# Query projection in seven products for eight, G products between FFN units, and a planning pass for ScalarE and VectorE in a linear-attention and FFN kernel

## The chip, the cores and the metric

The kernel runs on one core of one Trainium2 chip. Its inputs are in the chip's memory and its output goes back there. The metric is device time in microseconds (us) from one launch to its end; each figure below that is called a time is such a time, and a span is the stretch from the first to the last instruction of one profiled execution.

## The reference: what is computed

One block of 2048 tokens of width 640 in bf16. The input is normalised; a linear attention with 32 heads of width 20 and an FFN of width 1728 both read the normalised input, and their product is added to the input.

```python
phi = lambda t: jnp.where(t > 0, t + 1, jnp.exp(t)) + 1e-6
xn = _layernorm(x, axis=-1)
q, k, v = split_heads(xn @ wqkv)              # 32 heads of 20
pq, pk = phi(q), phi(k)
kv = jnp.einsum("bhsd,bhse->bhde", pk, v)     # per head, 20 x 20
z = jnp.einsum("bhsd->bhd", pk)
num = jnp.einsum("bhqd,bhde->bhqe", pq, kv)
den = jnp.einsum("bhqd,bhd->bhq", pq, z)[..., None] + 1e-6
s = merge_heads(num / den) @ wo
g = silu(jnp.maximum(xn @ w1, 0) @ w2)
out = x + s * g
```

## The kernel before, in words

Tokens are cut into 16 tiles of 128 (t) and 4 chunks of 512 (j); the width 640 is 5 blocks of 128, the FFN width 13 blocks of 128 and one of 64. The values are never projected: since kv is a sum over tokens, the kernel first makes G = xn^T pk (640 x 640), then kv = wv^T G with a mask for the heads, and then W = kv wo, which is called wf. An output tile is then pq (divided by the denominator) times wf, times the gate g, plus x.

*Stages.* (1) Head: load x, mean and variance on VectorE (`bn`, `aggr`), the inverse root on POOL (`aggr`, L475 and L477), normalised tiles xn on VectorE (L497), transposed into xnT by transfers on SP; key tiles 0 to 7 and the FFN blocks 4, 5, 10, 11, 12 of chunk 0. (2) Middle: key tiles 8 to 15 (`K_mm` L556, exp and relu on ScalarE L569, sum on VectorE in `K_fin`), query blocks (`Q_mm` L609: 128 columns of wq by a chunk; exp L617 and relu L622 on ScalarE, sum L630 and L827 on VectorE), FFN blocks (`H_mm` L658) and FFN units. (3) G, kv and wf. (4) The eight pairs of output tiles: the second FFN product with its gate (`U_steps`), the attention product (`O_steps` or, for tiles 0, 1, 14 and 15, `s_tile` and `s_last` at L1529), multiply (L1517), add of x (L1522) and store.

*Seven products for eight.* A 2 x 2 block product needs eight block products, or seven in the scheme of Strassen and Winograd, which takes four sums of the left and four of the right operand ahead of it and combines results in PSUM after it. `h_unit` (L1036 for the matmuls) does this for the FFN: blocks i and i + 6, two chunks, inner dimension 4 of the 5 blocks; the fifth block is added as plain products, so a unit has 18 matmuls of 512 columns for 20. There are four units for chunks 0 and 1 and six for chunks 2 and 3. `seven` (matmuls at L882, copies at L889) does it for G (two pairs of row blocks, the fifth row block by 32 plain matmuls at L1580), for the second FFN product and for the attention product. Steps of a unit are called s1, s5, s6, s2, s7, s3, s4; between them ScalarE copies results from one PSUM bank to another (L1042, L889) and VectorE adds (L827). A unit holds four of the eight PSUM banks. The sums of the left and right operands are made on VectorE by `h_S`, `h_T`, `g_S`, `g_T1` to `g_T4`, `u_S`, `u_T`, `o_S`, `o_T`; they all call `tt`, L827.

*The denominator.* `z_sum` (L756) and `z_col` (L774) make the sums of the keys, `den` (L786) multiplies all queries by them, VectorE scales it (L790) and takes four reciprocals (`den_rec`, L799). `den_store` (L806) writes them spread out to a buffer scr in the chip's memory, four transfers of 640 KB, one for each chunk; `load_recip` (L815) reads them back, and `divide` (L820) multiplies the queries by them. wf is assembled by ten small transfers on SP (L1335) from tiles that ScalarE and VectorE copied out of PSUM (L1325, L1328).

*What sets the order.* All instructions go through `Sched`. `op`, `group` and `dma` put an instruction, or a group of matmuls with one semaphore count at its end, at the end of its engine's queue, and work out from the keys that it reads and writes what it must wait for. Each engine runs its queue in that order. Before the change the order on every engine is the order of the calls, written out by hand: two FFN units take turns on the two halves of PSUM, with query blocks, plain FFN blocks and key tiles as filling between their steps (`fill_`, `misc`, `qfill`); G's units stand after the last FFN unit.

Of the kernel before, what the change touches and what calls it, by code (L numbers as in the profile page):

```python
# [11 lines left out]
class _Res:  # L12
    __slots__ = ("w", "r", "nread")

    def __init__(self):
        self.w = None
        self.r = {}
        self.nread = 0


class Sched:

    def __init__(self, nc, n_dma_sems):
        self.nc = nc
        self.ops = {E: [] for E in ENGS}
        self.count = {E: 0 for E in CENGS}
        self.gseq = 0
        self.seq_at = {E: [] for E in CENGS}
        self.seq_at_dma = []
        self.vc = {E: {} for E in ENGS}  # L30
        self.vc_at = {E: [] for E in CENGS}
        self.vc_at_dma = []
        self.res = {}
        self.ndma = 0
        self.dma_sem_of = []
        self.dsem_count = [0] * n_dma_sems
        self.dsem_last_k = [None] * n_dma_sems
        self.n_dma_sems = n_dma_sems
        self.allow_unread = set()

# [18 lines left out]
    def _require(self, E, agents, waits):  # L59
        need_eng = {}  # L60
        need_dma = []
        for a in agents:
            if self._known(E, a):
                continue
            if a[0] == "D":
                if a not in need_dma:
                    need_dma.append(a)
            else:
                if need_eng.get(a[0], -1) < a[1]:
                    need_eng[a[0]] = a[1]  # L70
        items = [("E", Ep, idx, self.seq_at[Ep][idx]) for Ep, idx in need_eng.items()] + \
                [("D", a[1], None, self.seq_at_dma[a[1]]) for a in need_dma]
        items.sort(key=lambda x: -x[3])
        for kind, a1, a2, _sq in items:
            if kind == "E":
                Ep, idx = a1, a2
                if self._known(E, (Ep, idx)):
                    continue
                waits.append(("E", Ep, idx + 1))
                vc = self.vc[E]  # L80
                vc[Ep] = max(vc.get(Ep, 0), idx + 1)
                self._merge(E, self.vc_at[Ep][idx])
            else:
                k = a1
                if self._known(E, ("D", k)):
                    continue
                si, val = self.dma_sem_of[k]
                waits.append(("D", si, val))
                self.vc[E][("D", k)] = True
                self._merge(E, self.vc_at_dma[k])  # L90

    def _hazards(self, R, W):
        agents = []
        for key in R:
            st = self.res.get(key)
            if st is not None and st.w is not None:
                agents.append(st.w)
        for key in W:
            st = self.res.get(key)
            if st is not None:  # L100
                if st.w is not None:
                    agents.append(st.w)
                agents.extend(st.r.values())
        return agents

    def _update_res(self, agent, R, W):
        Rset = set(R)
        for key in R:
            st = self.res.get(key)
            if st is None:  # L110
                st = self.res[key] = _Res()
            rk = agent if agent[0] == "D" else agent[0]
            st.r[rk] = agent
            st.nread += 1
        for key in W:
            st = self.res.get(key)
            if st is None:
                st = self.res[key] = _Res()
            else:
                assert (st.w is None or st.nread > 0 or key in Rset or key in self.allow_unread  # L120
                        or (agent[0] == "PE" and st.w[0] == "PE")), (
                    "unread overwrite of %r by %r (prev writer %r)" % (key, agent, st.w))
            st.w = agent
            st.r = {}
            st.nread = 0

    def op(self, E, fn, R=(), W=(), extra=()):
        return self.group(E, [fn], R, W, extra)

    def group(self, E, fns, R=(), W=(), extra=()):  # L130
        assert E in CENGS
        waits = []
        agents = self._hazards(R, W) + list(extra)
        self._require(E, agents, waits)
        idx = self.count[E]
        self.count[E] += 1
        self.vc_at[E].append(dict(self.vc[E]))
        self.seq_at[E].append(self.gseq)
        self.gseq += 1
        self.ops[E].append(("op", waits, fns, idx))  # L140
        self._update_res((E, idx), R, W)
        return (E, idx)

    def dma(self, E, fn, sem_idx, R=(), W=(), extra=()):
        waits = []
        agents = self._hazards(R, W) + list(extra)
        prev = self.dsem_last_k[sem_idx]
        if prev is not None:
            agents.append(("D", prev))
# [14 lines left out]
    def wait_all_dma(self, E, sem_idxs):  # L164
        waits = []
        for si in sem_idxs:
            k = self.dsem_last_k[si]
            if k is None:
                continue
# [1527 lines left out]
```

## Time and profile before

| | |
|---|---|
| time, median of 3 runs | 209.08 us (208.42 to 210.09) |
| span of the profiled execution | 207.0 us |
| PE (TensorE matmul) busy | 203.6 us, 98% |
| DVE (VectorE) busy | 169.7 us, 82% |
| ACT (ScalarE) busy | 124.3 us, 60% |
| POOL (GpSimd) busy | 18.0 us, 9% |
| moved by DMA | 24.74 MB |
| query blocks, L609 | 100 matmuls |
| FFN units, L1036 | 180 matmuls |
| seven-product units, L882 | 612 matmuls |

The profiled execution's own time is not given apart from its span; the three times shown are of other executions of the same program. In the profile, PE is TensorE's matmuls, PEld its weight loads (beside the matmuls), DVE VectorE, ACT ScalarE, POOL GpSimd, and SP the engine whose queue issues most transfers. A line number is a line of the kernel. A matmul's entry lasts longer than the distance to the next one, since matmuls overlap; a stretch divided by the matmuls in it gives what one costs. The chain that ended last is followed back from the last instruction; a wait is put down to what released it.

### The profile page before, as it was taken

How to read it: one execution, taken by the hardware profiler on the slowest of the kernel's cores; microseconds unless marked ns; L12 is line 12 of the kernel's file. 1: busy time of each engine (PE TensorE's matmuls, PEld its weight loads, DVE VectorE, ACT ScalarE, POOL GpSimd, SP SyncE). 2: the span in 40 equal slices, each digit the busy share in tenths (PEclk: the TensorE clock that was granted, in tenths of full speed). 3: DMA queues.
4: the chain of work that ended last, by engine and by line, in shares of the span. 5: the costliest groups of instructions: out<-in, count | busy, mean ns of one | idle time of the engine just before them, and what ended most of it. 6: DMA issues, size and time to landing. Idle time of an engine off the chain costs nothing.

```text
span 207.0 us, 3745 instructions
## 1 busy us (share of the span) xinstructions
PE 203.6 (98%) x1400; PEld 126.3 (61%) x1400; DVE 169.7 (82%) x373; ACT 124.3 (60%) x251; POOL 18.0 (9%) x53
## 2 busy tenths in 40 slices
PE   8999999999999999999999999999999999999995
PEld 7755645545555444444456777777777777777773
DVE  4888997988969787686889669898888989897465
ACT  5598869888889987686563435462525354352531
POOL 3174032101330000000000000000000000000001
PEclk9999999999999999999999999999999999999999
DMA  6965999211037000302225999237931011010103
GB/s 194 331 190 117 255 203 275 42 32 29 6 63 198 25 3 0 127 0 57 74 63 114 251 357 384 90 108 234 371 129 63 3 63 46 21 63 0 63 5 127
DMA packets 32999, 24.74 MB, mean 119 GB/s; under 512 B 12757, under 2 KB 32981, under 8 KB 32981
## 3 DMA queue, kind: packets, MB, share of 16 engines
q1 hardware_dynamic: 31749, 23.13, 39.2%
q10 hardware_dynamic: 1232, 1.37, 1.9%
q8 instruction: 11, 0.18, 0.4%
q14 instruction: 7, 0.06, 0.1%
HBM read 15.81 MB, written 5.24 MB: 102 GB/s over the span
## 4 chain that ended last, share of the span: by engine, by line
PE 97%; DMA 1%; DVE 1%; issue 0%
PE psT L882 40%; PE psT L1036 19%; PE psT L556 11%; PE psT L609 11%; PE psT L658 6%; PE psT L1529 3%; PE psT L1580 2%; DMA reg<-in_A_x_dram 1%; PE psT L676 1%; PE psT L1320 1%; PE psT L530 1%; PE psT L1294 1%; PE psT L756 1%; PE psT L786 1%; PE psT L432 0%; DVE stats L469 0%
## 5 line engine op out<-in xcount | busy, mean ns | idle before, releaser
L882 PE MATMUL psT<-reg,regH 128*128 128x320 bf16 (+1 forms) x224 | 34.3, 299 | 0.0
L882 PE MATMUL psT<-reg 128*128 128x320 bf16 (+1 forms) x164 | 27.7, 299 | 0.0
L882 PEld LDWEIGHTS psT<-reg,regH 128*128 128x128 bf16 (+1 forms) x224 | 21.9, 98 | 8.6
L1354 ACT ACTIVATE wv_sb<-psT 128x320 bf16<-128x320 f32 x28 | 11.3, 436 | 25.2 <-PE psT L882 15.4
L609 PE MATMUL psT<-reg 128*128 128x512 bf16 x100 | 24.4, 379 | 0.0
L1036 PE MATMUL psT<-reg 128*128 128x512 bf16 x80 | 23.2, 379 | 0.0
L827 DVE TENSOR_TENSOR psT<-psT,reg 128x320 f32<-128x320 f32 x30 | 14.3, 493 | 9.3 <-PE psT L882 9.2
L889 ACT ACTIVATE psT<-psT 128x320 f32<-128x320 f32 x32 | 13.6, 426 | 11.2 <-PE psT L882 10.7
L882 PEld LDWEIGHTS psT<-reg 128*128 128x128 f16 (+1 forms) x164 | 16.0, 98 | 6.9 <-DVE regH L827 0.2
L889 ACT ACTIVATE reg<-psT 128x320 f32<-128x320 f32 (+1 forms) x24 | 10.4, 435 | 15.6 <-PE psT L882 13.6
L556 PE MATMUL psT<-reg 128*128 128x320 bf16 x120 | 17.9, 299 | 0.0
L1042 ACT ACTIVATE psT<-psT 128x512 f32<-128x512 f32 x20 | 11.9, 595 | 8.2 <-PE psT L1036 8.2
L569 ACT ACTIVATE regE<-psT 128x640 bf16<-128x640 f32 x24 | 15.6, 706 | 1.9 <-PE psT L556 1.2
L609 PEld LDWEIGHTS psT<-reg 128*128 128x128 bf16 x100 | 9.6, 98 | 11.6 <-issue 0.7
L1048 ACT ACTIVATE regH<-psT 128x512 bf16<-128x512 f32 (+1 forms) x24 | 14.5, 604 | 2.1 <-PE psT L1036 1.8
L556 PEld LDWEIGHTS psT<-reg 128*128 128x128 bf16 x120 | 11.5, 98 | 6.5 <-ACT regE L569 0.5
L469 DVE BATCH_NORM_STATS2 stats<-reg 128x6 f32<-128x320 bf16 x32 | 14.1, 475 | 1.3 <-DMA reg<-in_A_x_dram 1.3
L827 DVE TENSOR_TENSOR reg<-reg 128x1024 f16<-128x1024 bf16 (+6 forms) x17 | 13.5, 805 | 1.7 <-DMA reg<-in_B_w_dram 1.2
L882 PE MATMUL psT<-reg,pqT 128*128 128x320 bf16 (+1 forms) x72 | 14.7, 299 | 0.0
L1517 DVE TENSOR_TENSOR reg<-psT,wv_sb 128x640 bf16<-128x640 f32 (+2 forms) x16 | 11.8, 739 | 3.0 <-PE psT L882 1.8
L1036 PEld LDWEIGHTS psT<-reg 128*128 128x128 bf16 x80 | 7.7, 98 | 9.4 <-issue 0.4
L1522 POOL TENSOR_TENSOR reg<-reg 128x224 bf16<-128x224 bf16 x1 | 0.6, 607 | 144.0 <-DVE reg L1517 144.0
(143 smaller groups left out, 369.0 us busy)
## 6 DMA issues: line engine op xcount, KB each, us to landing
reg<-in_B_w_dram SPq DMA_DIRECT2D x12, 320.0 KB, 5.5
scr<-rden SPq DMA_DIRECT2D x4, 640.0 KB, 8.3
reg<-in_A_x_dram SPq DMA_DIRECT2D x4, 640.0 KB, 6.6
out_dram<-reg SPq DMA_DIRECT2D x15, 160.0 KB, 1.9
regE<-scr SPq DMA_DIRECT2D x3, 640.0 KB, 7.5
reg<-in_A_x_dram SPq DMA_DIRECT2D x4, 320.0 KB, 4.4
reg<-in_A_wo_dram SPq DMA_DIRECT2D x6, 160.0 KB, 3.3
reg<-in_A_x_dram SPq DMA_DIRECT2D x5, 160.0 KB, 5.5
```

Source lines behind the costliest of these rows:

```text
L469: sc.op("DVE", lambda eng: eng.bn_stats(stats[:, t, a, :], xv[:, HN * a:HN * (a + 1)]), R=[("xin", xs(t))], W=[("stats", t, a)])
L556: fns.append(lambda eng, a=a, k=k, lhs=lhs: eng.matmul(ps[b + a][:, 0:HN], lhsT=lhs, rhs=wk[:, k, HN * a:HN * (a + 1)], start=(k == 0), st ...
L569: sc.op("ACT", lambda eng: eng.activation(out=o_.rearrange("p (a n) -> p a n", a=2), in_=ps2(b, HN), func=func, scale=scale), R=[("ps", b) ...
L609: sc.group("PE", [(lambda eng, k=k: eng.matmul(ps[b], lhsT=wq[:, k, P * f:P * (f + 1)], rhs=xnT[:, j, k, :], start=(k == 0), stop=(k == C ...
L658: sc.group("PE", [(lambda eng, k=k: eng.matmul(ps[b], lhsT=w1_col(k, P * f, P), rhs=src[:, k, :], start=(k == 0), stop=(k == C - 1))) for ...
L827: sc.op("DVE", lambda eng: eng.tensor_tensor(out=out, in0=in0, in1=in1, op=op), R=R, W=W, extra=extra)
L882: sc.group("PE", [(lambda eng, k=k, lhs=lhs, rhs=rhs: eng.matmul(ps[b][:, 0:HN], lhsT=lhs, rhs=rhs, start=(start and k == 0), stop=(k == n ...
L889: sc.op("ACT", lambda eng: eng.activation(out=dst, in_=ps[b][:, 0:HN], func=ACTF.Copy), R=[("ps", b)], W=[dkey], extra=extra)
L1036: sc.group("PE", [(lambda eng, k=k, lhs=lhs, rhs=rhs: eng.matmul(ps[b], lhsT=lhs, rhs=rhs, start=(start and k == 0), stop=(k == n - 1), sk ...
L1042: sc.op("ACT", lambda eng: eng.activation(out=dst, in_=ps[b], func=ACTF.Copy), R=[("ps", b)], W=[dkey], extra=extra)
L1048: sc.op("ACT", lambda eng: eng.activation(out=dst, in_=ps[b], func=ACTF.Relu), R=[("ps", b)], W=[("hT", j, f)])
L1517: sc.op("DVE", lambda eng: eng.tensor_tensor(out=tmpo[:, os_, lo:hi].rearrange(shp, a=na), in0=src, in1=g_of(t)[0][:, lo:hi].rearrange(shp ...
```

## The change

1. *Query blocks.* A new `q_unit(f, jp)` makes query blocks f and f + 2 of chunks 2jp and 2jp + 1 in seven products. `h_unit` is split into a common `unit` and its own output rules, and `q_unit` uses the same `unit`: four units take the place of 16 of the 20 query blocks. Four sums of wq are made once (`q_S`), in a part of the hidden buffer that is not yet written. The sums of xnT for both halves of the tokens (`h_T`) now have buffers of their own, the second in the buffer of the input tiles.
2. *G.* The two G units stand between FFN units, and the fifth row block of G is in two parts (`c0`, `c1`), one ahead of the last G unit. Some buffers move with it (`gT4`, the sums of G's second pair, the denominator).
3. *Key tiles 8 to 15* are made by halves of 320 columns in one bank each (`K_half`), with their own exp and relu; the filler matmuls of 192 columns (`whole`, L562) are gone.
4. *Order.* TensorE's order after the head is a written list of steps, `PROGRAM`, of which `a` and `b` are FFN units, `p` and `q` query units, `g` G units, `u` and `o` the second FFN product and the attention product. A step takes free PSUM banks as it comes. `Sched` first records everything; `place` then runs through the program with assumed durations (`cost`, `LAT`, `RATE`), works out for each operation how late it may be for TensorE to keep its order, and fixes the order on ScalarE, VectorE and POOL: of the first 60 recorded operations whose inputs are there, the one that can start first, or one that is due earlier. TensorE and SP keep the recorded order, and the head keeps its own on all engines. `emit` then works out the waits.
5. *Loads.* The load of wv is in two parts, wo is loaded after the FFN units (its buffer now holds sums of xnT till then), the last pair of w2 after the last FFN unit, the stores and reloads of the reciprocals behind them on SP, x for the final add behind the last reload. The denominator's product stands later, after the last FFN unit.
6. *Output.* Tile 14's attention product stands after the last FFN product, right ahead of tile 15's.

The core of the diff:

```diff
-    def h_unit(i, jp=1):
+    def unit(jp, blk, wkeys_, ws, skeys, out, out22, tile=None):
...
+    def q_unit(f, jp):
+        o = P * f
+
+        def out(half, j, b):
+            both, sum_ = Q_evac(j, f + 2 * half, b)
+            both()
+            pend.append(sum_)
+
+        def out22(j, b, s5, skey):
+            tt(ps[b], ps[b], s5, ALU.add, [("ps", b), skey], [("ps", b)])
+            out(1, j, b)
...
+    def K_half(t, a):
+        b = take(True)
+        K_mm(t, [b, b], halves=(a, ))
+        for func, slot, key in ((ACTF.Exp, 0, "ek_e"), (ACTF.Relu, 1, "ek_r")):
...
-        if whole:
-            fns.append(lambda eng: eng.matmul(ps[b][:, HN:512], lhsT=one, rhs=wk[:, 0, 0:512 - HN], start=False, stop=True,
-                                              skip_group_check=True))
...
+    LAT = {"PE": 0.2, "ACT": 0.07, "DVE": 0.07, "POOL": 0.07, "SP": 0.0}
+    RATE = 300e3
...
+    if E == "POOL":
+        return 0.25, 0.3
...
+        for o in reversed(recs):
+            run = o.dur + (o.byt / self.RATE if o.byt else 0.0)
+            o.late = min([recs[s].late - run - self.LAT[o.E] for s in o.succ] + [goal.get(o.n, end - run)])
...
+                    can = [(max(free[E], ready[o.n]), o.late, o.n) for o in w[:self.LOOK] if not nleft[o.n]]
+                    if not can:
+                        continue
+                    est, late, n = min(can)
+                    c = recs[n]
+                    for e2, l2, n2 in can:
+                        if l2 < c.late and (e2 <= est or (e2 < est + c.occ and l2 < est + c.occ)):
+                            c, est2 = recs[n2], e2
...
+PROGRAM = """
+H15 H14 H112 rb LN8 H111 T0 Q04 SQ a0.s5 LN12 a0.s1 H110 SH1 Ka8 a0.s6 a0.s2 p1.s1 p1.s5 a0.s7 a0.s3 p1.s2
+a0.s4 Kb8 p1.s6 Kb9 Ka9 p1.s7 p1.s3 a1.s1 Q14 a1.s5 Ka10 T1 a1.s6 a1.s2 p1.s4 Kb10 a1.s7 hh0 Kb12 a1.s3 a1.s4
...
+q0.s4 b2.s5 g0.s6 g0.s2 g0.s7 b2.s1 g0.s3 b2.s6 b2.s2 zc w2a g0.s4 b2.s7 b4.s5 b4.s1 b2.s3 mv6 b2.s4 b4.s6
+b5.s1 b5.s5 w2b b4.s2 b4.s7 b5.s6 b4.s3 b5.s2 b4.s4 c0 hh1 b5.s3 GS1 w2d g1.s1 b5.s7 g1.s5 b5.s4 w2c dn g1.s6
+g1.s2 g1.s7 wo sl wv1 uSa0 g1.s3 do uSb0 g1.s4 wv0 c1 rc1 uT1 dv0 u0.s1 uT3 uT2 kv0 uT4 kv1 u0.s5 W5 u0.s6
+uSa2 W3 W2 u0.s2 W0 u0.s3 W1 u0.s7 u1.s1 uSa1 W4 dv1 oT u1.s5 u1.s6 u1.s2 u0.s4 uSb1 rc2 oS2 u1.s7 uSb2 u1.s3
+u1.s4 rc3 xre st1 u2.s1 oS1 st0 uSa3 u2.s5 o1.s1 u2.s6 dv3 o1.s5 o1.s2 o1.s6 u2.s2 uSb3 o1.s7 o1.s3 dv2 u2.s7
...
+o6.s5 u7.s2 o6.s2 o6.s6 u7.s7 o6.s7 o6.s3 u7.s3 o6.s4 u7.s4 st14
+"""
...
+    def wo_load():
+        for c in range(VC):
+            r0 = VR * c if c < VC - 1 else D - P
+            dma("SP", lambda eng, c=c, r0=r0: eng.dma_start(wo_sb[:, c, :], A_wo[r0:r0 + P, :]),
+                W=[("wo", c)], extra=norms + hz(hTk))
+
+    def den_out():
+        den_store(0)
+        den_store(1)
+        load_recip(0)
+        den_store(2)
+        den_store(3)
```

In the list, `w2c` and `wo` are loads, `dn` the denominator's product with its reciprocals, `do` the function `den_out`, `rc1` to `rc3` the further reloads, `W0` to `W5` the blocks of wf, `dv` the divides, `st1`, `st0` and `st14` output tiles, `xre` the reload of x.

## The prediction, made before the changed kernel was run

> **What bounds the kernel now.** I read the page's busy shares first, then the chain of work that ended last in order of time, then the busy time of each engine by stage, then the DMA queue of SP.
>
> ```profile
> span 207.0 us, 3745 instructions
> ...
> PE 203.6 (98%) x1400; PEld 126.3 (61%) x1400; DVE 169.7 (82%) x373; ACT 124.3 (60%) x251; POOL 18.0 (9%) x53
> ...
> PE 97%; DMA 1%; DVE 1%; issue 0%
> ```
>
> TensorE carries 97% of the chain. A busy PE could still be a stalled one, so I divide the chain's shares by the counts: L1036 (FFN units, 512 columns) has 18.8% of 207.0 us for 180 matmuls, 216 ns each; L882 (320 columns) 40.2% for 612, 136 ns; L609 (query blocks, 512) 10.5% for 100, 217 ns. Each long group costs the same everywhere, so from 4.5 us to 204.5 us TensorE hardly waits: 200 us of matmuls, 4.5 us ahead, 2.5 us behind. What takes no matmul away cannot help by more than those ends.
>
> ```profile
> 34.97 0.08 PE psT L562
> ...
> 200.82 1.36 PE psT L1529 x10
> 202.18 0.95 PE psT L882 x7
> 203.12 1.39 PE psT L1529 x15
> 204.51 0.02 issue
> 204.53 0.38 DVE reg L1517
> 204.92 0.02 issue
> 204.94 0.37 DVE reg L1522
> ```
>
> (Chain: start, length, what.) The end: tile 14's ten matmuls, a last FFN product, tile 15, then one multiply, one add and the store.
>
> ```profile
> 23.60:90.00 66.40, 66.40 (x385) 32.98 (x383) 55.28 (x140) 54.85 (x102) 8.30 (x22) 1.00 0.37 89
> 90.00:117.00 27.00, 27.00 (x189) 14.55 (x188) 23.07 (x37) 15.62 (x30) 0.00 (x0) 1.00 0.33 83
> 117.00:142.00 25.00, 25.00 (x206) 18.35 (x204) 20.11 (x33) 11.61 (x24) 0.00 (x0) 1.00 0.70 231
> 142.00:207.00 65.00, 62.50 (x465) 45.10 (x463) 52.29 (x112) 24.75 (x65) 0.61 (x1) 1.00 0.26 91
> ```
>
> (Stage: length, then busy PE, PEld, DVE, ACT, POOL, clock, DMA share, GB/s.) VectorE and ScalarE are 83% busy in the first stage while TensorE does not wait: there is room, but little. The clock is 1.00 throughout.
>
> ```profile
> SPq L815 <- DMA scr<-rden: 2.8, 1, 2.8
> ...
> DMA to landing us min/median/max: 5.0/7.7/10.4
> ...
> L1335 SPq DMA_DIRECT2D reg<-reg x10: 552/739/991, 132.5 to 139.4; - x10
> ```
>
> (SP's waits; landing of the transfers of scr; the ten copies that assemble wf.) SP stands still until the reciprocals have landed in scr, and each copy of wf holds it 0.74 us.
>
> **The change, part by part.** Times are of the one profiled execution, span 207.0 us; its own total is not given. The median of the three runs is 2.1 us over the span, which I take to stay.
>
> *Matmuls removed.* Sixteen of the 20 query blocks (80 matmuls at L609) become four units of 18 (72): 8 x 0.216 = 1.73 us. The four 192-column fillers at L562 go: 4 x 0.08 = 0.32 us. Every other matmul is kept, only moved. All of it lies on the chain: -2.05 us.
>
> *Work added beside it.* Each query unit adds three ScalarE copies (row L1042, 0.60 us) and two VectorE adds (row L827, 512 from PSUM, 0.70 us), and four sums of wq at 0.42 us are made once: ScalarE +7.2 us, VectorE +7.3 us. Key tiles 8 to 15 are evacuated by halves, 4 x 0.44 for 2 x 0.71 us: ScalarE +2.8 us. These hide beside TensorE if they fit. In the first 66.4 us of the changed part (it starts at 23.6 us) VectorE had 55.3 us; about 7.0 of the 7.3 us and three G sums of 1.48 us come in: 66.7 us. The three G sums and some 2 us of other G operands are not needed until later, so 60 to 62 us are due, 93% of the stretch. With 83% the wait was nil; at over 100% it would be a microsecond or more.
>
> *The pass.* It fixes each engine's order by times that it assumes. It assumes 0.3 us for a POOL operation; rows L475 and L477 show 0.28 and 0.62 us. So a normalisation may be placed about 0.3 us before its input is there, and what stands behind it on VectorE (the adds that free PSUM) waits too. Eight tiles are open to this: at most 2.4 us of VectorE idle (the row of before shows 1.6 us in four waits). For both effects on TensorE the bounds are 0 (all absorbed) and 3 us; I take 0.4, near the row of before, which cost nothing.
>
> *The loads moved.* TensorE's order is written out in the program, so I added its matmuls up at 136 and 216 ns. The last w2 pair is issued after the last FFN unit, 117.1 us, and needed at 125.6; wo is queued behind it, needed at 128.9; the first part of wv waits for the same unit and is needed at 126.5. Landing was 5.5 (7.7 at most) for w2, 3.3 for wo, 9.0 for all 800 KB of wv, of which this part is 320. All have 8.5 us or more: nothing, and up to 1 us if that cover is gone.
>
> *The reciprocals and SP's queue.* The denominator product moves from 97.4 to 98.5 us to end at 118.0 us, while the first output tile stays at about 142 (141.9 by the sums). Behind it: 0.2 to reach VectorE, 0.69 (L790), 3.5 for four reciprocals (L799): 122.4 us. Then SP has, in this order: stores 0 and 1, reload 0 (waits for store 0), stores 2 and 3, reload 1 (waits for store 1), the ten copies of wf. Store 0 landed 5.6 us after issue before (109.8 to 115.4); so reload 0 at 128.0, issued in 1.6 us, two stores in 1.4, reload 1 in 0.4: 131.4. Ten copies at 0.74: 138.8; the last lands 2.2 later, oT needs 0.49 and the tile about 0.1 more: 141.6, against 141.9. One reciprocal set back by another VectorE operation of 0.7 us uses that up. By the largest row (10.4 for 5.6) it is 4.8 us more. Bounds 0 and 4.5 us; I take 0.5, since the first store is the one whose row applies. The divide, late next, has more room: reload 0 lands 7.4 after 128.0, divide 1.64: 137. Behind reload 3, which waits for divide 1 (reload 1 at 131.4 + 7.4, divide 1.64: 140.5), SP issues the loads of xre; the first lands 6.6 later, about 148, and the adds that read it stand on VectorE. Three buffers hold products until the fourth output tile at 152.8: nothing, up to 2 us if an add stands too early.
>
> *The end.* Tile 14 now stands right ahead of tile 15. Its multiply (0.82) and add (0.48) no longer fall under the 0.95 us FFN product: multiply 14 ends 0.4 us before the last matmul, two multiplies of tile 15 (0.3 each) follow, then add 14, the last multiply (0.38) and add (0.37): the last add ends about 1.3 us after TensorE, where it was 0.8. +0.5 us; bounds 0 (add 14 goes last and its store lands under the other) and 0.9.
>
> *Sum.* -2.05 + 0.4 + 0.5 + 0.5 = -0.65 us: span 206.35, time 208.4 us.
>
> **The rivals.**
>
> *SP's queue holds the first output tile (slower than before).* It decides as soon as reload 1 is issued after about 131.7 us; each later microsecond costs one. For it: the 5.0/7.7/10.4 row, and the 2.8 us for which SP stood before. Against it: the reloads' issue took 0.37 us at the median of three, where I count 1.6. With a store of 8.5 to 10.4 us it costs 2.9 to 4.8 in place of 0.5: 210.8 to 212.7 us.
>
> *VectorE becomes the bound of the first stage.* At 62 us due and the idle of before (11.1 of 66.4 us) cut only by half, 67.6 us are needed for 66.4; with the POOL waits up to 70. It costs 1.2 to 4 in place of 0.4: 209.2 to 212.0 us. Against it: the pass may take any ready operation out of 60, and query sums can be put off.
>
> *Nothing waits.* The hand-made order shows that these engines can be kept behind TensorE; then -2.05 us, 207.0 us. Since 200 us of matmuls less 2.05 are left whatever the order, much less is not possible.
>
> *The clock falls after a long wait.* The opening fillers (L432) loaded weights for 32 matmuls of 128 columns in 3.34 us, 104 ns each; five transposes of the same width later took 0.28 us, 56 ns each: TensorE is at half rate after idling. If the first output tile waits nearly 5 us, a stretch like that one returns and adds 1.7 us: 212.7 + 1.7 = 214.4. [...]
>
> That the change does not do what it says can be left out: the four query units stand in the written program with all their steps.
>
> **How the numbers follow.** Forecast case (small waits, 207.4 to 209.4) 0.58; nothing waits 0.07; VectorE 0.14; SP's queue 0.18; queue and clock 0.03. A measurement here tells about 1% from no change, 207.0 to 211.2 us. Faster needs less than the matmuls allow, so it takes most of the "nothing waits" case and luck: 0.05. Slower: two thirds of the queue's case, the clock, and half of VectorE's: 0.22. The rest, 0.73, is within 1%. The range runs from 206.8 to 212.0 us and leaves out some 0.03 below and 0.09 above; the forecast case alone spans 207.4 to 209.4.
>
> **What would show it.** Right: 1388 matmuls (8 and 4 fewer), chain shares that still give 216 and 136 ns, VectorE over 90% busy in the first 66 us after 23.6, a gap of half a microsecond or none just ahead of the first output tile, and an end some 3 us behind the last matmul. Wrong: TensorE groups with idle ahead of them that name VectorE in the first stage, a copy of wf as the releaser of a gap of over 2 us, a clock under 1.00, or a w2 or wv load as a releaser at 125 us.

## The result, and the profile after

The changed kernel takes 221.68 us (median of four runs, 219.29 to 222.82) where the kernel before takes 208.91: 1.058 times as long, with an interval of 1.051 to 1.065 (a ratio is worked out from the executions, not from the two medians). An execution that fell in a slower state of the chip (here the one of 222.82) is left out of the ratios, and out of the two medians further down that are said to be of three. The forecast was 208.4, within 206.8 to 212.0. The profiled execution has a span of 220.4 us, 13.4 more than before.

The page of the changed kernel:

```profile
span 220.4 us, 3735 instructions
...
PE 206.0 (93%) x1376; PEld 125.1 (57%) x1388; DVE 170.6 (77%) x385; ACT 131.4 (60%) x279; POOL 17.9 (8%) x53
...
PE   8899972999999999999999999959999999999994
...
PEclk9999997699999999999999999997999999999999
...
PE 59%; DMA 15%; DVE 12%; ACT 6%; issue 3%; POOL 2%; SPq 1%; DVEq 0%
```

There are 12 matmuls fewer, as announced (1388 weight loads; some matmul records are missing). But TensorE has fallen from 97% of the chain to 59%, and DMA has risen from 1% to 15%. The slices (5.5 us each) show two holes, in the slices from 33 and from 143 us, and the clock goes down with each. TensorE's waits (line, releaser: us in total, times, longest) and four stretches (length, then busy PE, PEld, DVE, ACT, POOL, clock, DMA share, GB/s):

```profile
PE psT L690 <- DMA reg<-reg: 4.8, 1, 4.8
PE psT L997 <- DVE reg L941: 2.3, 1, 2.3
PE psT L690 <- DMA reg<-in_A_wqkv_dram: 0.9, 1, 0.9
```

```profile
23.60:35.00 11.40, 8.07 (x40) 3.44 (x39) 10.29 (x27) 7.09 (x13) 2.96 (x10) 1.00 1.12 269
35.00:45.00 10.00, 7.76 (x26) 3.37 (x28) 4.22 (x12) 4.38 (x9) 1.82 (x4) 0.66 0.29 47
45.00:90.00 45.00, 44.64 (x246) 22.29 (x249) 39.58 (x98) 40.50 (x90) 3.42 (x8) 1.00 0.12 24
...
142.00:155.00 13.00, 10.73 (x67) 6.98 (x66) 9.16 (x18) 4.19 (x10) 0.00 (x0) 0.87 0.86 260
```

From 45 to 90 us, where most steps of the query units stand, TensorE is 99% busy: the stage that the forecast worried about is not where the time went. A clock of 0.66 over 10 us is 6.8 us at half rate (it reads 0.50 from 35.4 to 42.3 us), of which TensorE worked some 5: 2.5 us lost behind the 4.8 of the wait. A clock of 0.87 over 13 us is 3.4 us at half rate (0.50 from 148.1 to 151.5): 1.7 lost behind the 2.3.

*The first hole.* The chain of the changed kernel (start, length, what):

```profile
26.47 2.71 DMA reg<-reg
...
30.52 6.62 DMA reg<-reg
...
37.19 1.51 PE psT L690 x5
38.70 4.20 PE psT L1170 x11
```

Two transposing transfers (reg<-reg). The one at 26.47 landed in 2.7 us; the one at 30.52 is tile 8's, took 6.6, and key tile 8 (`Ka8`, L690) waits for it. What SP issued ahead of it, in the changed kernel and then in the kernel before:

```profile
23.75 4.00 SPq L679 DMA_TRANSPOSE reg<-reg  x3
27.79 1.60 SPq L513 DMA_DIRECT2D reg<-in_A_x_dram  x3
29.44 1.04 SPq L518 DMA_DIRECT2D reg<-in_B_w_dram  x2
30.52 4.71 SPq L679 DMA_TRANSPOSE reg<-reg  x2
```

```profile
27.48 0.58 SPq L374 DMA_DIRECT2D reg<-in_A_x_dram  x1
28.10 1.21 SPq L546 DMA_TRANSPOSE reg<-reg  x1
29.36 1.11 SPq L374 DMA_DIRECT2D reg<-in_A_x_dram  x2
30.51 1.04 SPq L379 DMA_DIRECT2D reg<-in_B_w_dram  x2
```

Before, tile 8's transposition (28.10) went ahead of the last input tiles and two parts of w1. In the change it is recorded with `LN8`, behind them: 2.4 us later in the queue, and behind 1.3 MB more (four transfers of 320 KB). Its input was there in time; VectorE's normalisation of tile 8 in the changed kernel:

```profile
27.63 0.45 DVE L630 TENSOR_SCALAR reg<-reg,mv,rsy 128x640 bf16<-128x640 bf16 x1
```

*The second hole.* The chain again, 100 us later:

```profile
132.95 5.01 DMA scr<-rden
...
137.98 6.73 DMA reg<-scr
...
144.72 1.56 DVE pqT L934 x2
146.28 0.73 DVE reg L1589
147.02 0.54 DVE reg L941
...
147.61 6.62 PE psT L997 x35
```

Store 0, reload 0, divide 0, a block of wf, then one operand sum (L941, `uSa1`), and only then u1.s5, the second step of the second FFN product. The waiting step does not use the divided queries at all. By the code, `uSa1` writes into the buffer that reload 0 filled, so it must wait until divide 0 has read that.

*The end.* In the changed kernel VectorE has two adds (L1778, the first of them tile 14's) and a multiply left to do after TensorE (L1785, tiles 14 and 15):

```profile
214.22 2.89 PE L1785 MATMUL psT<-reg,pqT 128*128 128x320 bf16 x25
...
217.10 0.83 DVE L1778 TENSOR_TENSOR reg<-reg 128x640 bf16<-128x640 bf16 x1
217.86 0.36 DVE L1773 TENSOR_TENSOR reg<-psT,wv_sb 128x208 bf16<-128x208 f32 x1
218.26 0.38 DVE L1778 TENSOR_TENSOR reg<-reg 128x416 bf16<-128x416 bf16 x1
```

From the last matmul (its entry ends at 217.1) to the end of the span it is 3.3 us, where it was 2.5. The add of tile 14 takes 0.83 us here; the adds of the same size just ahead of it (at 213.5 and 214.7) take 0.48 and 0.49.

### The profile page after: what moved, and what is told of

It is laid out like the page before. It is cut to its first block, busy times and chain, and to the rows that moved or that the text cites. A ratio compares the mean times of both kernels' runs of the same rounds, so it can differ in the third digit from the quotient of the medians.

```text
span 220.4 us, 3735 instructions
## 1 busy us (share of the span) xinstructions
PE 206.0 (93%) x1376; PEld 125.1 (57%) x1388; DVE 170.6 (77%) x385; ACT 131.4 (60%) x279; POOL 17.9 (8%) x53
## 4 chain that ended last, share of the span: by engine, by line
PE 59%; DMA 15%; DVE 12%; ACT 6%; issue 3%; POOL 2%; SPq 1%; DVEq 0%
PE psT L997 26%; PE psT L1170 23%; PE psT L690 4%; DMA reg<-reg 4%; DMA reg<-in_A_x_dram 3%; DMA reg<-scr 3%; DMA reg<-in_A_wqkv_dram 3%; DMA scr<-rden 2%; DVE pqT L934 2%; DVE stats L611 2%; DVE reg L941 1%; PE psT L741 1%; POOL rsy L619 1%; ACT regE L1446 1%; PE psT L793 1%
## 5 line engine op out<-in xcount | busy, mean ns | idle before, releaser
L1170 PE MATMUL psT<-reg 128*128 128x512 bf16 (+1 forms) x139 | 38.6, 388 | 0.4
L997 PE MATMUL psT<-reg,regH 128*128 128x320 bf16 (+1 forms) x224 | 35.3, 301 | 0.6 <-DVE reg L1773 0.4
L997 PE MATMUL psT<-reg 128*128 128x320 bf16 (+1 forms) x172 | 29.1, 303 | 2.3 <-DVE reg L941 2.3
L997 PEld LDWEIGHTS psT<-reg,regH 128*128 128x128 bf16 (+1 forms) x224 | 22.0, 99 | 9.9 <-DVE reg L1773 0.8
L1004 ACT ACTIVATE psT<-psT 128x320 f32<-128x320 f32 x32 | 13.4, 425 | 17.8 <-PE psT L997 15.2
L1170 PEld LDWEIGHTS psT<-reg 128*128 128x128 bf16 (+1 forms) x144 | 14.2, 100 | 17.1 <-issue 1.4
L690 PE MATMUL psT<-reg 128*128 128x320 bf16 x120 | 19.3, 306 | 4.8 <-DMA reg<-reg 4.8
L941 DVE TENSOR_TENSOR psT<-psT,reg 128x320 f32<-128x320 f32 (+1 forms) x33 | 16.6, 512 | 9.1 <-PE psT L997 7.7
L997 PEld LDWEIGHTS psT<-reg 128*128 128x128 f16 (+1 forms) x172 | 16.8, 98 | 10.5 <-DVE reg L941 2.6
L1004 ACT ACTIVATE reg<-psT 128x320 f32<-128x320 f32 (+1 forms) x24 | 10.6, 443 | 18.8 <-PE psT L997 14.7
L690 PEld LDWEIGHTS psT<-reg 128*128 128x128 bf16 x120 | 11.5, 99 | 12.5 <-DMA reg<-reg 5.3
L941 DVE TENSOR_TENSOR reg<-reg 128x1024 f16<-128x1024 bf16 (+6 forms) x24 | 17.1, 722 | 1.9 <-PE psT L1460 1.3
L1177 ACT ACTIVATE psT<-psT 128x512 f32<-128x512 f32 x28 | 17.1, 621 | 1.4 <-PE psT L1170 1.4
L941 DVE TENSOR_TENSOR psT<-psT,wv_sb 128x512 f32<-128x512 f32 x15 | 10.4, 695 | 9.6 <-PE psT L1170 9.5
L1446 ACT ACTIVATE regE<-psT 128x320 bf16<-128x320 f32 x32 | 12.3, 461 | 6.5 <-PE psT L690 6.5
L997 PE MATMUL psT<-reg,pqT 128*128 128x320 bf16 (+1 forms) x72 | 14.3, 299 | 0.0
L1778 POOL TENSOR_TENSOR reg<-reg 128x224 bf16<-128x224 bf16 x1 | 0.6, 606 | 163.4 <-DVE reg L1773 163.4
L1773 DVE TENSOR_TENSOR reg<-psT,wv_sb 128x640 bf16<-128x640 f32 (+2 forms) x16 | 11.6, 735 | 2.4 <-PE psT L997 1.7
L752 ACT ACTIVATE regE<-psT 128x512 bf16<-128x512 f32 x20 | 11.9, 631 | 2.2 <-PE psT L741 1.2
```

The lines of the kernel that those rows point to most:

```text
L690: fns.append(lambda eng, a=a, k=k, lhs=lhs: eng.matmul(ps[bk[a]][:, 0:HN], lhsT=lhs, rhs=wk[:, k, HN * a:HN * (a + 1)], start=(k == 0), st ...
L752: exps.append(sc.op("ACT", lambda eng: eng.activation(out=e_, in_=ps[b], func=ACTF.Exp), R=[("ps", b)], W=[("er_e", es)]))
L941: sc.op("DVE", lambda eng: eng.tensor_tensor(out=out, in0=in0, in1=in1, op=op), R=R, W=W, extra=extra)
L997: sc.group("PE", [(lambda eng, k=k, lhs=lhs, rhs=rhs: eng.matmul(ps[b][:, 0:HN], lhsT=lhs, rhs=rhs, start=(start and k == 0), stop=(k == n ...
L1004: sc.op("ACT", lambda eng: eng.activation(out=dst, in_=ps[b][:, 0:HN], func=ACTF.Copy), R=[("ps", b)], W=[dkey], extra=extra)
L1170: sc.group("PE", [(lambda eng, k=k, lhs=lhs, rhs=rhs: eng.matmul(ps[b][:, 0:nn], lhsT=lhs if tile is None else rhs, rhs=rhs if tile is Non ...
```

## The experiments

Each was timed beside the kernel before, which took 208.4 to 209.2 us; all ratios are to it. A run's time is the median of four executions, or of three where that is said.

### 1. Tile 8's transposition ahead of the loads

```diff
-    x_load(12, 2)
+    LN_norm(8), x_load(12, 2)
...
-        "LN8": lambda: run([(N, 8), (S, 9), (N, 9), (S, 10), (N, 10), (S, 11), (N, 11)]),
+        "LN8": lambda: run([(S, 9), (N, 9), (S, 10), (N, 10), (S, 11), (N, 11)]),
```

> Only SP's order differs from the changed kernel: the transposition of token tile 8 is issued ahead of the loads of x tiles 12 to 15 and two parts of w1, as in the kernel before. Theory 'queue': the 4.8 us for which TensorE waited at 32 us and the half clock behind it (about 2.5 us) go, 221.7 - 7.3 = 214.4 us. Rival 'full engines': VectorE and ScalarE (10.0 and 9.6 of 10 us busy from 55 to 65) cannot follow an earlier TensorE, the wait comes back by 70 us, and at most 3 us are won: 218.7 us or more.

Measured: 214.72 us, ratio 1.031 (1.024 to 1.038). One transposition moved in one queue gives back 7.0 us, about the 4.8 of the wait and the 2.5 of the half clock; the rival ("full engines") falls. Tile 8's transposition is issued at 27.7 and lands 3.6 us later. The second hole is as it was: TensorE's longest wait, and the clock down for 3.4 us behind it.

```profile
PE psT L997 <- DVE reg L941: 2.9, 1, 2.9
```

### 2. The pass told what the transfers really take

The pass assumes about 2 us and the bytes at 300 GB/s for a transfer. Here a store to scr is given a least time of 5.5 us (stores 0 and 1) or 8.0, and a reload 7.0; alone, and together with experiment 1. The order changes on VectorE.

```diff
-                    c.end = line[0] + 0.4
+                    c.end = max(line[0] + 0.4, est + c.floor)
...
-            run = o.dur + (o.byt / self.RATE if o.byt else 0.0)
+            run = max(o.dur + (o.byt / self.RATE if o.byt else 0.0), o.floor)
```

> Only VectorE's order differs: the planning pass is told that a store to scr takes 5.5 or 8.0 us and a reload 7.0 us, as the traces show, so it places the divide later. Theory 'fixed order': VectorE no longer stands 2.7 us in front of the divide with the sums for TensorE behind it, and the wait of 2.3 us at 145 us and the half clock behind it (1.7 us) go: 221.7 - 4.0 = 217.7 us. Rival 'next in line': the first output tile waits for the divide or for wf anyway, and little is won: 220.5 us or more.

> Both edits. If the two waits are apart and nothing else takes their place: 221.7 - 7.3 - 4.0 = 210.4 us. Rival 'full engines': 215 us or more.

Measured: 222.68 us alone, 1.063 (1.056 to 1.070), and 216.85 with the transposition moved, 1.038 (1.035 to 1.041): no gain, rather 1 to 2 us lost, which the intervals do not clearly separate from nothing. u1.s5 still waits 3.0 us. VectorE with the transposition moved:

```profile
138.24 0.82 DVE L1589 CAST reg<-psT 120x640 bf16<-120x640 f32 x1 [0.27 <-PE psT L1584]
138.98 1.55 DVE L934 TENSOR_TENSOR pqT<-pqT,reg 128x1536 bf16<-128x1536 bf16 x2
```

Reload 0 goes out at 130.8 and lands 7.1 us later, at 137.9; the pass has now put both of VectorE's copies of wf (L1589) ahead of divide 0, which therefore starts at 139.0. So VectorE's order has about 1 us of this wait. The other 2 us are the buffer of reload 0: TensorE was at u1.s5 at 138.2, and divide 0 (1.56) with one sum of `uSa1` (0.6) behind a landing at 137.9 ends at 140.1 in any order. The theory that VectorE's fixed order holds `uSa1` falls for that part.

### 3. The denominator earlier

`dn` put ahead of the last step of unit b4, in three forms. First with all four stores right behind it, reload 0 behind the last w2 pair (all these runs include experiment 1):

```diff
-b5.s1 b5.s5 w2b b4.s2 b4.s7 b5.s6 b4.s3 b5.s2 b4.s4 c0 hh1 b5.s3 GS1 w2d g1.s1 b5.s7 g1.s5 b5.s4 w2c dn g1.s6
-g1.s2 g1.s7 wo sl wv1 uSa0 g1.s3 do uSb0 ...
+b5.s1 b5.s5 w2b b4.s2 b4.s7 b5.s6 b4.s3 b5.s2 dn do b4.s4 c0 hh1 b5.s3 GS1 w2d g1.s1 b5.s7 g1.s5 b5.s4 w2c rc0 g1.s6
+g1.s2 g1.s7 wo sl wv1 uSa0 g1.s3 uSb0 ...
```

> Tile 8's transposition ahead of the loads, and the denominator's product with its four reciprocals and stores put ahead of the last step of FFN unit b4, reload 0 behind the last w2 pair. If the wait of 2.9 us ahead of u1.s5 and the half clock behind it come from the chain denominator, store, reload, divide (theory 'chain'), both go: 214.7 - 2.9 - 1.7 = about 210.1 us, clock 1.00. If VectorE or the next load in line (wf's copies, xre, the first output tile) takes their place (rival 'next in line'), a wait of 2 us or more stands within some 15 us of the old one and the time is 213 us or more.

Measured: 222.50 us, 1.065 (1.057 to 1.072), 8 us worse than experiment 1. The wait ahead of u1.s5 is gone; another is there. TensorE's longest wait in this run, and SP's queue:

```profile
PE psT L997 <- DMA reg<-in_B_w_dram: 9.2, 1, 9.2
```

```profile
118.29 5.82 SPq L920 DMA_DIRECT2D scr<-rden  x4
124.16 2.16 SPq L1069 DMA_DIRECT2D reg<-in_B_w_dram  x1
126.36 4.25 SPq L1074 DMA_DIRECT2D reg<-in_B_w_dram  x2
130.66 2.20 SPq L1069 DMA_DIRECT2D reg<-in_B_w_dram  x2
```

SP stood for the reciprocals until 118.3 and then issued 2.6 MB of stores; the last w2 parts (L1074, then L1069), at 115.9 and 119.8 in experiment 1, went out 10 to 11 us later, and the first FFN product waited for them. The rival was right.

Then only store 0 early, and behind the last w2 pair; and then all stores behind wo, so that only the product and the reciprocals are earlier:

```diff
+...b5.s2 dn b4.s4 ... b5.s4 w2c ds0 g1.s6 ... wo sl wv1 uSa0 do g1.s3
```

```diff
+...b5.s2 dn b4.s4 ... b5.s4 w2c g1.s6 ... wo sl wv1 uSa0 do g1.s3
```

> Tile 8's transposition ahead of the loads, the denominator's product ahead of the last step of unit b4 (reciprocals done at about 118), but of the stores only store 0 early, and behind the last w2 pair on SP: issued at about 120.7 us where it was 126.0; it lands at about 126, reload 0 about 133 where it was 138.4. If the wait ahead of u1.s5 hangs on this chain alone (theory), it and its half clock go: 214.7 - 2.9 - 1.7 = about 210.1 us. If any byte ahead of the first FFN product's loads costs as much as it saves (rival: the transfers are the bound here), TensorE waits 2 us or more for a w2 load at about 126, or for the denominators again, and the time is 213 us or more.

> As the run before it (store 0 behind the last w2 pair), but all four stores behind wo, as in the changed kernel: only the denominator's product and the reciprocals are earlier. Store 0 at about 123.6 us where it was 126.0, so reload 0 lands some 2.4 us earlier, and of the wait of 2.9 us some 0.5 is left: theory 210.5 to 212.5 us (the half clock goes unless the last half microsecond brings it). Rival (reciprocals not the start of the chain): the wait stays at 2 to 3 us, 214 to 215 us.

Measured: 215.55 us, 1.028 (1.022 to 1.034), and 214.51, 1.027 (1.022 to 1.031). TensorE's waits in the first and in the second (L997 is u1.s5; L1784 and L1785 are the first output tile):

```profile
PE psT L1784 <- DVE reg L941: 3.0, 1, 3.0
```

```profile
PE psT L1785 <- DVE reg L941: 1.6, 1, 1.6
PE psT L997 <- DVE reg L941: 1.5, 1, 1.5
```

Whole, or in halves: about 3 us of waiting stay, at u1.s5 (2.9 in experiment 1), at the first output tile (3.0), or at both. In the first run reload 0 goes out at 128.8 and u1.s5 does not wait, but store 1 then goes out at 129.2, reload 1 at 136.7, divide 1 follows at 145.4, and the sums for the first output tile stand behind it on VectorE; the clock is down for 3.4 us behind that wait.

### 4. A quarter of the denominators' bytes

This changes the last run of experiment 3 (214.51 us). Each store writes 160 rows for 640 and each reload reads one block of five, which the divide uses for all five; the order is the same on every engine, and the result is not the reference's.

```diff
-        src = rden[H * i:H * (i + 1), :].unsqueeze(1).to_broadcast([H, DH, 512])
+        src = rden[H * i:H * i + 8, :].unsqueeze(1).to_broadcast([8, DH, 512])
...
-        dma("SP", lambda eng: eng.dma_start(Rr[r], scr[:, schunk(i)].rearrange("(m p) s -> p m s", p=P)),
+        dma("SP", lambda eng: eng.dma_start(Rr[r][:, 0:1, :], scr[0:P, schunk(i)].rearrange("(m p) s -> p m s", p=P)),
```

> As the run with the denominator's product early and the stores behind wo (214.5 us), with the same order on every engine, but a quarter of each store and a fifth of each reload of the denominators is moved (160 rows for 640, one block of five), and the divide uses that one block for all five: the output is not the reference's. Theory (the bytes of the denominators in the stretch from 120 to 155 us hold what is left): the two waits of 1.6 and 1.5 us go, 211.0 to 211.9 us. If the dependency costs by its steps and not by its bytes (rival), one of the waits stays at over 1 us: 213 or more.

Measured: 215.18 us, 1.031 (1.027 to 1.035). The theory falls: the denominators' own bytes are not what is left. VectorE of this run (divide 0, then the operands for the first output tile, which wait for a copy of wf):

```profile
136.04 1.56 DVE L934 TENSOR_TENSOR pqT<-pqT,reg 128x1536 bf16<-128x1536 bf16 x2 [0.36 <-DMA reg<-scr]
...
147.70 0.89 DVE L941 TENSOR_TENSOR reg<-reg 128x640 f16<-128x640 bf16 x2 [1.76 <-DMA reg<-reg]
```

Divide 0 starts 1.1 us earlier than with all bytes (137.2), and u1.s5's wait of 1.5 goes (0.5 is left at the step behind it), but the first output tile waits 1.8. Store 0, at a quarter of its size, was still 5.8 us from issue (125.5) to the issue of reload 0 (131.4): 1.6 MB of w2 and wo had been issued in the 4 us ahead of it. Whether these hold it was not tried.

### 5. The copies of wf ahead of reload 1; all blocks of wf on ScalarE

Both change the last run of experiment 3 too.

```diff
-... wv0 c1 rc1 uT1 ... W4 dv1 oT u1.s5
+... wv0 c1 uT1 ... W4 oT rc1 dv1 u1.s5
```

```diff
-        if c in (1, 4):
+        if c in ():
             sc.op("DVE", lambda eng: eng.tensor_copy(dst, ps2(b, HN)[0:n]), R=[("ps", b), ("ps", b + 1)],
```

> As the run with the denominator's product early and the stores behind wo (214.5 us), with reload 1 and divide 1 behind the ten copies of wf instead of ahead of them. Theory (the 1.6 us ahead of the first output tile are SP's order: the copies stand behind reload 1, which waits for store 1): the copies start at about 135.5 and not 137.6, the wait of 1.6 us goes, and 212.9 us is left. Rival (two blocks of wf wait on VectorE behind divide 0, so the copies cannot end earlier, or divide 1 now holds the next tiles): one wait of over 1 us between 139 and 160 stays beside the first, 214 us or more.

> As the run with the denominator's product early and the stores behind wo (214.5 us), with all six blocks of wf copied out of PSUM by ScalarE instead of four by ScalarE and two by VectorE. Theory (the first output tile waits because two blocks of wf stand on VectorE behind divide 0): the last copy of wf is issued some 2 us earlier, the wait of 1.6 us goes, and u1.s5, which stood behind one of those blocks on VectorE, waits 0.7 us less: 212.2 to 212.9. Rival (the copies are late because SP stands behind reload 1): the wait ahead of the first output tile stays at over 1 us, 213.5 or more.

Measured: 216.65 us, 1.040 (1.037 to 1.042), and 214.28 (median of three), 1.031 (1.023 to 1.039). Neither helps. TensorE's waits in the first, and in the second with tile 14 moved (experiment 6; in the profile without that the clock was down for 6.8 us):

```profile
PE psT L997 <- DVE reg L941: 1.8, 1, 1.8
PE psT L997 <- DVE reg L1773: 1.3, 1, 1.3
...
PE psT L1785 <- DVE reg L941: 0.7, 1, 0.7
```

```profile
PE psT L997 <- DVE reg L941: 3.0, 1, 3.0
...
PE psT L1785 <- DVE reg L941: 0.7, 1, 0.7
```

With the copies first, the first output tile waits 0.7 for 1.6, but what stands behind the copies on SP comes later (the loads of x for the adds at 152.2 and not 147.8), and a wait of 1.3 us follows behind a multiply (L1773); the copies begin at 134.3 but still end at 145.5. So neither SP's order nor VectorE's blocks of wf hold the stretch by themselves. What the runs of experiments 4 and 5 share with their base is store 0 at 125 us and divide 0 at 136 to 139.

### 6. Tile 14 ahead of the last step of u7, as before

Tried on five kernels: experiment 2 with the transposition moved, the first form of experiment 3, experiment 4 and both of experiment 5.

```diff
-... o6.s7 o6.s3 u7.s3 o6.s4 u7.s4 st14
+... o6.s7 o6.s3 u7.s3 o6.s4 st14 u7.s4
```

> Both edits, and tile 14 ahead of the last FFN product again, as in the kernel before. Theory: the end behind TensorE's last matmul falls from 3.4 us to the 2.5 us of before, 0.9 us under the run with both edits: 209.5 us. Rival: the end is set by the store's landing and differs by less than 0.3 us.

> As the run with the denominator moved (about 210.1 us), with tile 14's attention product ahead of the last step of FFN unit u7, as in the kernel before. If tile 14's multiply and add then lie under the last product (theory), the stretch behind the last matmul falls from about 3.4 to 2.6 us and the time by 0.5 to 0.9: 209.4. If the waits just ahead absorb it (rival), it is within 0.3 us of that run.

> As the run with a quarter of the denominators' bytes (about 211.4 us; output not the reference's for the same reason), with tile 14's attention product ahead of the last step of unit u7. Theory: the stretch behind the last matmul falls by 0.5 to 0.9 us and the time with it, to 210.7. Rival: the time is the same within 0.3 us.

> As the run with the copies first (212.9 us), with tile 14's attention product ahead of the last step of unit u7. Theory: the stretch behind the last matmul falls from 3.3 to 2.5 us, 212.1. Rival: the time is the same within 0.3 us.

> As the run with all blocks of wf by ScalarE (212.5 us), with tile 14's attention product ahead of the last step of unit u7. Theory: the stretch behind the last matmul falls from 3.3 to 2.5 us, 211.7. Rival: the time is the same within 0.3 us.

Measured: 216.89 us (1.037, 1.032 to 1.041), 221.99 (1.063, 1.059 to 1.068), 213.48 (1.025, 1.022 to 1.028), 215.31 (1.033, 1.029 to 1.038) and 213.84 (1.025, 1.019 to 1.031). Against the same kernel without it: 0.0, -0.5, -1.7, -1.3 and -0.4 us, -0.8 in the mean. In the profiles of the third pair the stretch behind the last matmul is 2.5 us for 3.2, so 0.7 is tile 14's; single pairs lie up to 1 us off that either way, and what made the rest was not traced. The last, at 213.84, is the best version that computes the reference: it is still 2.5% slower than the kernel before.

### 7. Plain query blocks again; no pass

The 16 query blocks as plain products, at the steps s2, s7, s3 and s4 of the units that they replace: on the first form of experiment 3, on its last form, and on experiment 4. And on that first form the pass with a view of one operation.

```diff
-a0.s4 Kb8 p1.s6 Kb9 Ka9 p1.s7 p1.s3 a1.s1 Q14 a1.s5 Ka10 T1 a1.s6 a1.s2 p1.s4 Kb10 ...
+a0.s4 Kb8 Kb9 Ka9 Q03 Q11 a1.s1 Q14 a1.s5 Ka10 T1 a1.s6 a1.s2 Q13 Kb10 ...
```

```diff
-    LOOK = 60
+    LOOK = 1
```

> As the run with the denominator moved (about 210.1 us), but the 16 query blocks are plain products again, 80 matmuls for 72, without the sums of wq, the copies and the adds of the four units. If TensorE is the bound and the eight matmuls count (theory), it is 8 x 0.216 = 1.7 us slower than that run, about 211.8. If the units' work on ScalarE and VectorE in the first stage costs as much as the matmuls save (rival), it is equal or faster: 210.1 or less, with shorter waits on ScalarE or VectorE between 24 and 90 us.

> As the run with the denominator's product early and the stores behind wo (214.5 us), but the 16 query blocks are plain products again: 80 matmuls for 72, no sums of wq, no copies and adds of the units. Theory (TensorE is the bound in the first stage, so the matmuls count): 8 x 0.216 = 1.7 us slower, 216.2. Rival (the run that was 8 us slower without the units showed a real cost of plain blocks, their two exps and relus standing in bursts): 3 us or more slower, 217.5 or more, with waits for ScalarE or VectorE between 30 and 90 us. Third: not slower, 214.5 or less.

> As the run with a quarter of the denominators' bytes (about 211.4 us; output not the reference's for the same reason), with the 16 query blocks as plain products again. With nothing waiting at the denominators, theory: 1.7 us slower than that run, 213.1. Rival: 3 us or more slower. Third: not slower.

> As the run with the denominator moved (about 210.1 us), but ScalarE, VectorE and POOL run in the recorded order behind the head: the planning pass looks at one operation and not at 60. If the pass is needed for this program (theory), TensorE waits for VectorE or ScalarE at many places, 5 to 20 us more: 215 to 230. If the recorded order is good enough by itself (rival), within 2 us of that run: 208 to 212.

Measured, plain blocks: 230.77 us (1.103, 1.094 to 1.112), 221.27 (median of three; 1.067, 1.061 to 1.074) and 219.04 (1.053, 1.049 to 1.057), so 8.3, 6.8 and 3.9 us slower than with the units. By their count the matmuls are 1.7 of that; the wait lists show new waits beside it. The largest of the third run is not at the query blocks but 40 us behind them, at kv (L1558), whose last part of wv ScalarE issued at 129.3 us and not at 121.8, where the whole run stands some 3 us later:

```profile
129.31 0.39 ACTq L518 DMA_DIRECT2D wv_sb<-in_A_wqkv_dram  x1
```

```profile
135.73 1.59 PE L1558 MATMUL psT<-reg,wv_sb 128*128 128x120 bf16 x30 [2.14 <-issue]
```

The reason is again a buffer. ScalarE copies a result of the last G unit (L1004) to one of the places that take turns, in this run and then in experiment 4:

```profile
124.21 0.44 ACT L1004 ACTIVATE wv_sb<-psT 128x320 f32<-128x320 f32 x1 [0.51 <-PE psT L997]
```

```profile
120.86 0.44 ACT L1004 ACTIVATE reg<-psT 128x320 f32<-128x320 f32 x1 [0.51 <-PE psT L997]
```

With the four units gone, the turn falls on the place in wv's buffer; VectorE has read it at 129.3, and then the load goes out. The second run has the same (a wait of 3.3 us at kv). So these 2.1 and 3.3 us are not the price of plain blocks; that price by itself stays open, and nothing contradicts 1.7 us. Without the pass: 278.01 us (1.330, 1.322 to 1.339), beyond the 230 that was expected. This written order needs it.

## Why the prediction was wrong

From the forecast's span without its additions, 204.95 us, to the 220.4 of the profile:

| step | forecast | measured |
|---|---|---|
| matmuls | -2.05 | 12 fewer; not isolated |
| first stage | +0.4 | 0.3 in waits for ScalarE; 1.2 for it and VectorE in experiment 1 |
| loads moved | 0 | +7.0 (experiment 1), the transposition behind them |
| denominators | +0.5 | +4.0: wait 2.3, half clock 1.7 |
| end | +0.5 | +0.8 |

204.95 + 7.0 + 4.0 + 0.8 = 216.75; of the other 3.65 us, the wait list names 2.7 (0.9 for a load in the head, which is 0 to 0.8 in the profiles of the experiments, 0.5 ahead of the first query block, and five smaller ones); 0.95 is not traced.

*"The loads moved: nothing."* This step failed, and it is the larger half. It followed the loads that the description of the change names (w2, wo, wv) to the places where each is needed. It did not list what SP issues in the first 35 us, in the old and the new order. There one line of the diff puts a transposition, needed at 32.4 us, 4.3 after its input was ready, behind 1.3 MB of loads; with these sent after it, in experiment 1, TensorE waits for none of them. The pass could not repair that, since SP keeps the recorded order; and the forecast had no rival with SP in the first stage.

*"The divide, late next, has more room."* This failed too. The chain's own durations were close: in experiment 1 the reciprocals took 3.4 (forecast 3.5), store 0 took 5.0 (5.6), reload 0 took 7.4 (7.4); it all ran some 3 us later, mostly because the product ended at 120.9 and not 118.0. But the deadline was taken from the reader of the divided queries, the first output tile at 141.9. The first to need divide 0 is the writer of its buffer, `uSa1`, and through it u1.s5, which TensorE had reached at 138.4 in experiment 1. A buffer reused is a deadline; it was not looked up. The forecast's own figures show the miss: 49 matmuls of 136 ns lie between u1.s5 and the first output tile, so TensorE is there at about 135.2 by its sums, where divide 0 ends at 137 and a block of wf (0.7) and a sum (0.6) follow it: an estimated wait of 3 us, which experiment 1 has at 2.9.

*SP's queue and the first output tile.* The rival was sound as a mechanism: a wait on u1.s5, some 8 us ahead of the first output tile (experiment 1), hides it. It comes out where that wait is taken away: 3.0 us in the second run of experiment 3, the low end of the 2.9 to 4.8 that it was priced at. Its sum was too short. From the issue of reload 0 to the end of the ten copies of wf the forecast had 10.8 us (128.0 to 138.8); it took 15.0 in experiment 1 (131.0 to 146.0) and in the last run of experiment 3 (131.4 to 146.4), since SP spent 2.6 and 3.5 us on the two stores where 1.4 were counted, 2.3 and 2.1 on reload 1 for 0.4, and 9.3 and 8.8 on the copies for 7.4; what it waited for in each is not worked out here. The first output tile before and in experiment 1:

```profile
142.38 1.52 PE L1529 MATMUL psT<-reg,pqT 128*128 128x320 bf16 x10
```

```profile
149.50 1.52 PE L1785 MATMUL psT<-reg,pqT 128*128 128x320 bf16 x10
```

It starts at 148.0 to 149.5 in the profiles of experiment 1, the second and last runs of experiment 3, experiment 4 and the first run of experiment 5, wherever the waits ahead of it stand.

*First stage and VectorE.* Right in kind. In the last run of experiment 3, VectorE is busy 59.9 of the 66.4 us from 23.6 on (90%; the forecast had 60 to 62 due), and TensorE waits there for VectorE and ScalarE in pieces of 0.5 us and less. (ScalarE's 2.8 us for the halves of the key tiles is 2.7 by the rows given; no term of the sum hangs on it.)

*The end.* Right in kind, short in size: 0.8 for 0.5, near the upper bound. The order was the one forecast; tile 14's add took 0.83 us where 0.48 was counted.

*The clock.* The condition was wrong. A wait of "nearly 5 us" was thought to be needed; it fell behind one of 2.3 us. That length was the author's guess and not shown by the trace of before: TensorE's longest wait there is 0.8 us, and its granted clock reads 1.00 from the start, also where the opening's matmuls took 104 ns for 56. The price of 1.7 us for one such stretch was right.

*The chances.* Slower had 0.22, all from waits in two named places. The changed kernel moved nearly every transfer of SP, and only some were followed; that should have weighed as a case of its own.

What stays open: after experiment 1 some 6 us are left over the kernel before. They lie ahead of the first output tile, which starts some 6 to 7 us later than before; from it to the end of the span experiment 1 takes 63.5 us and the kernel before 64.7. About 3 of them are waits that follow from the denominators' late start (store 0 at 109.8 us before, at 118 to 126 in experiments 1, 3, 4 and 5); they change place and hardly size, since a step let go earlier meets the next wait on the same chain of stores, reloads and copies. By the code, a still earlier product is held by its buffers, in which the changed kernel keeps operand sums for FFN units, and the stores then meet the w2 loads on SP; a version with other buffers was not tried. Nor does any run take back the halves of the key tiles or G's new place, so what these cost or save alone is open.

## What to carry to other kernels

When a change rewrites an order, list each queue's issues before and after, side by side, for every stage, and not only for the transfers that the change speaks of: the 7 us sat in four lines of SP's queue. For each transfer that becomes later, ask who reads the data, and also who next writes the buffer that they lie in. When repairs move a wait of the same size from place to place, look for the common start of their chains, here one product that now stands some 22 us later.

## What the runs showed of the hardware

*The clock halved behind a wait of 2.3 us.* It was down for 3.4 us behind a wait of 2.3 us in the changed kernel and one of 2.9 in experiment 1, for 6.8 behind 4.8. In the changed kernel it reads 0.50 there, and the matmuls of 320 columns followed at 267 ns and not at 136 (seven from 149.0 us on). Behind a wait of 3.0 us it was down for 3.4 in the second run of experiment 3, and stayed at 1.00 in experiment 2 with the transposition moved (the matmuls of 320 columns behind that wait follow at 136 ns) and in the last run of experiment 6 (the mean of its profile is 1.00). So the length of a wait alone did not decide it in these runs. The fall itself came at different points: at 35.4 us, 3.0 us into the wait of 4.8, and at 148.1, 0.5 us behind the end of the one of 2.3. What sets it off was not tested. Executions of one kernel can differ by such a stretch (experiment 4: 213.45 at a clock of 1.00, and 215.1 to 215.4 at 0.99), but not every step is one: the second run of experiment 3 has 213.38 and 215.58, both at 1.00.

*Small transfers behind big ones.* Of the changed kernel's 16 transpositions the median landed in 2.6 us, and tile 8's, behind 1.6 MB of loads, in 6.6; a store of 160 KB took 5.8 us behind w2 and wo, and one of 640 KB at the same place 6.4. In these cases the size of a transfer said little about when it lands; what was issued in the 4 us ahead of it said more.
